# Attention and two MoE layers on one core: queries and keys of a pair interleaved on even and odd partitions

## The chip, the cores and the metric

One core of a Trainium2 chip runs the whole program. The metric is the device time of one execution in microseconds; 1132.95 us is the median of three runs before the change (1131.27, 1132.95 and 1136.18).

The engines are named as in the profile: PE multiplies matrices, DVE, ACT and POOL work on tiles, and SP issues most of the DMAs. [...]

## The reference

```python
def _attn_ref(q, k, v):                      # (4, 8, 576, 64) each, float32
    ...
    q_rot, k_rot = (rotate(q), rotate(k))    # x1*cos - x2*sin, x1*sin + x2*cos
    scores = scale * np.matmul(q_rot, k_rot.transpose(0, 1, 3, 2))
    scores = scores - np.max(scores, axis=-1, keepdims=True)
    attn = np.exp(scores)
    attn = attn / (np.sum(attn, axis=-1, keepdims=True) + 1e-09)
    return np.matmul(attn, v)

def _moe_ref(x, w_in, w_out, s, b):          # 2304 tokens, 512 -> 2048 -> 512
    r = np.maximum(x @ w_in, 0.0)
    return (s * (r * r) + b) @ w_out

def _moe2_ref(x, w_gate, w_val, w_out):      # 512 -> 1536 -> 512
    g = x @ w_gate
    return (g / (1.0 + np.exp(-g)) * (x @ w_val)) @ w_out
```

Attention's output, with the heads side by side, goes through the first layer and then through the second. The weights come as 64-bit floats and are decoded on the chip.

## The kernel before

**Precision.** Every 32-bit operand of a product is split into a high part (rounded to the PE's fast 32-bit format) and a low part (what is left). A product is then two or three matmuls: high by high, high by low, low by high.

**Attention** runs over 16 pairs of heads. For a pair p there are two jobs.

*Preparation* (`prep`, L425). SP loads the queries and keys of the two heads into a tile `x` (L392) and the values into `vr`. POOL applies the rotation in four instructions per pair: two products into a second tile `ry` (L486, L488), one product in place on `x` (L491), and the sum back into `x` (L494). (For pair 0 DVE does it, in three groups.) PE transposes the rotated `x` in three groups of three blocks (L514), so that queries lie on partitions 0 to 63 and keys on 64 to 127 of the PSUM tile `pst`. ACT writes the high part of each group into `qkhi` (L523), and DVE the low part into `qklo` (L525). Then SP copies the parts from SBUF to SBUF to where the score matmuls want them, ten "spreads" a pair (L547): into `a` (query high on the upper half of the partitions, query low on the lower half), `t` (key low above, key high below) and `kz` (key high above, zeros below). One matmul over 128 partitions of `a` and `t` then gives two of the three terms at once, and one of `a` and `kz` the third. Pairs 0 and 1 go without spreads: ACT and DVE write `a`, `t` and `kz` directly (L533, L536).

*The pair itself* (`pair`, L584). For each of nine blocks of 128 queries: four or eight score matmuls (L619), the row maximum on DVE (L622), the exponential on ACT (L626). Then, in three thirds, transposes of the exponentials (L680, L683), their high part on ACT (L688) and low part on DVE (L695), and the products with the values (L710, L712), whose result is stored to `x_d` (L731): high and low sums as two DMAs.

**The buffers that matter here.** `a`, `t`, `kz` exist twice, by the pair's parity, so the spreads of pair p can go only when the scores of pair p-2 are done. `qkhi` and `qklo` exist once: `qkhi` of pair p+1 can be written only when all ten spreads of pair p have landed. `ry` exists once, `x` twice, and `x` is free for a load when the transposes have read it.

**What sets the order.** The kernel records all operations with a duration, a priority and the buffers they take, and a list scheduler (`Schedule.run`, L70) emits them engine by engine in the order of its own clock. A pair's preparation has a priority of 2.4 pairs ahead, so the buffers decide when it comes. Once emitted, the order on an engine is fixed, and what the chip does later than the scheduler's clock said shows as a wait of the whole engine.

**The MoE layers** follow: first layer in five blocks of 512 or 384 tokens, second layer in three blocks, both with weights in a pool of slots: ten slots (`wa`) filled during attention and 22 (`WB`) that take the place of attention's tiles when these are given up.

## Time and profile before

| | us |
|---|---|
| median of three runs | 1132.95 |
| span of the profiled execution (first to last instruction) | 1130.5 |
| PE busy | 1103.6 |
| DVE busy | 801.2 |
| ACT busy | 591.0 |
| POOL busy | 193.0 |

The profile gives the profiled execution's span alone; the median of the runs is 2.45 us above it. The first matmuls of the MoE layers start at 305.0 us of the span, while attention's last pair runs out; the second layer's first activation is at 708.1 us. Matmuls overlap in the records, so a busy PE is not a PE at its peak, but an idle PE is idle.

How to read rows of waits: "PE ps_t L680 <- DVE qklo L525: 4.0, 2, 2.6" says that PE instructions of line 680 (they write tile `ps_t`) stood still for 4.0 us in total, twice, 2.6 us at the longest, until a DVE instruction of line 525 had ended. In a timeline the wait stands in brackets behind the instruction. Where one instruction waits for several events, the profile names the last one it knows of; a DMA named there can be another on the same queue.

### The profile page before, as it was taken

The page shows a single profiled execution, that of the slowest core. Times are in us where ns is not written, and L with a number is a line of the kernel's source. Part 1 is how long each engine was busy: PE and PEld are TensorE (multiplying, and loading weights), DVE is VectorE, ACT ScalarE, POOL GpSimd, SP SyncE. Part 2 cuts the span into 40 slices and gives each one's busy share as a digit, 9 for nine tenths or more (in the row PEclk, how much of TensorE's full clock was granted, in tenths as well). Part 3 has the DMA queues.
Part 4 walks back from the last instruction along what each step waited for, and adds up shares of the span by engine and source line. Part 5 has one row for each costly group of instructions (what it writes and reads, how often), then busy time and mean ns, then how long its engine had stood idle before and what let it go on. Part 6 is the DMA issues. An engine that isn't in the chain of part 4 may idle for free. (4 is left out here: it accounts for less than half of the span.)

```text
span 1130.5 us, 17993 instructions
## 1 busy us (share of the span) xinstructions
PE 1103.6 (98%) x6314; PEld 1006.8 (89%) x6314; DVE 801.2 (71%) x1391; ACT 591.0 (52%) x1199; POOL 193.0 (17%) x156
## 2 busy tenths in 40 slices
PE   8989989999999999999999999999999999999998
PEld 7889888989988788888899999999979999899986
DVE  5879788999979867868768764555565555655560
ACT  5979888889978845544554543322242222422230
POOL 6876775752210000000000000000000000000000
PEclk9899999999999999999999999999999999999999
DMA  5587978777375477576576766766646652666501
GB/s 117 128 208 175 240 184 213 175 184 185 89 235 185 128 227 235 177 238 225 198 241 212 254 224 207 245 204 204 210 160 220 196 195 97 196 229 197 181 10 46
DMA packets 185721, 211.16 MB, mean 187 GB/s; under 512 B 71824, under 2 KB 121120, under 8 KB 185632
## 3 DMA queue, kind: packets, MB, share of 16 engines
q1 hardware_dynamic: 183792, 209.23, 61.8%
q8 instruction: 50, 0.82, 0.3%
q10 hardware_dynamic: 1840, 0.79, 0.2%
q14 instruction: 39, 0.32, 0.1%
HBM read 142.07 MB, written 47.26 MB: 167 GB/s over the span
## 5 line engine op out<-in xcount | busy, mean ns | idle before, releaser
L1241 DVE TENSOR_TENSOR tmp<-hb,tmp 128x384 f32<-128x384 f32 x252 | 140.0, 557 | 113.3 <-PE hb L811 112.4
L811 PE MATMUL hb<-xh,w 128*128 128x384 f32 (+1 forms) x560 | 199.2, 356 | 1.0 <-DVE w L349 1.0
L809 PE MATMUL hb<-xh,w 128*128 128x384 f32 (+1 forms) x560 | 199.0, 355 | 0.3 <-DVE pl L695 0.3
L810 PE MATMUL hb<-xl,w 128*128 128x384 f32 (+1 forms) x560 | 198.8, 355 | 0.0
L809 PE MATMUL acc<-gh,w 128*128 128x512 f32 (+1 forms) x320 | 117.8, 368 | 0.0
L810 PE MATMUL acc<-gl,w 128*128 128x512 f32 (+1 forms) x320 | 117.6, 368 | 0.0
L811 PE MATMUL acc<-gh,w 128*128 128x512 f32 (+1 forms) x320 | 117.6, 367 | 0.0
L622 DVE TENSOR_REDUCE nm<-ps_s 128x1 f32<-128x576 f32 x144 | 108.0, 751 | 9.8 <-PE ps_s L619 8.6
L809 PEld LDWEIGHTS hb<-xh,w 128*128 128x128 f32 x560 | 105.1, 188 | 10.9 <-PE ps_t L683 0.5
L810 PEld LDWEIGHTS hb<-xl,w 128*128 128x128 f32 x560 | 105.1, 188 | 10.3
L811 PEld LDWEIGHTS hb<-xh,w 128*128 128x128 f32 x560 | 105.1, 188 | 9.8 <-DVE w L349 1.8
L626 ACT ACTIVATE e<-ps_s,nm 128x576 f32<-128x576 f32 x144 | 107.3, 746 | 8.4 <-DVE nm L622 7.8
L688 ACT ACTIVATE ph<-ps_t 128x512 fp32r<-128x512 f32 x192 | 106.2, 574 | 10.1 <-PE ps_t L680 7.8
L619 PE MATMUL ps_s<-t,a 128*128 128x288 f32 x320 | 101.2, 332 | 7.2 <-ACT e L626 7.0
L710 PE MATMUL ps_av<-ph,vh 128*128 128x384 f32 (+1 forms) x320 | 97.9, 327 | 0.7 <-ACT xr L723 0.6
L695 DVE TENSOR_TENSOR pl<-ps_t,ph 128x512 fp32r<-128x512 f32 x144 | 95.9, 683 | 2.5 <-ACT ph L688 1.4
L1256 ACT ACTIVATE tmp<-tmp 128x384 f32<-128x384 f32 x72 | 37.8, 525 | 111.1 <-DVE tmp L1241 108.9
L680 PE MATMUL ps_t<-ident,e 128*128 128x128 f32 x576 | 87.7, 279 | 5.6 <-DVE qklo L525 4.0
L619 PE MATMUL ps_s<-kz,a 128*128 128x288 f32 x320 | 90.8, 299 | 0.0
L810 PE MATMUL hb<-w 128*128 128x384 f32 x264 | 88.9, 337 | 0.0
L811 PE MATMUL hb<-w 128*128 128x384 f32 x264 | 88.8, 337 | 0.0
L809 PE MATMUL hb<-w 128*128 128x384 f32 x264 | 88.5, 335 | 0.0
(117 smaller groups left out, 2304.2 us busy)
## 6 DMA issues: line engine op xcount, KB each, us to landing
w<-wd SPq DMA_DIRECT2D x120, 512.0 KB, 4.3
wd<-w SPq DMA_DIRECT2D x48, 512.0 KB, 3.6
raw<-in_moe_w_out_dram SPq DMA_DIRECT2D x28, 512.0 KB, 4.1
x_d<-xr SPq DMA_DIRECT2D x64, 144.0 KB, 2.7
w<-wd SPq DMA_DIRECT2D x36, 256.0 KB, 3.6
raw<-in_moe_w_in_dram SPq DMA_DIRECT2D x16, 512.0 KB, 4.4
raw<-in_moe_w_gate_dram SPq DMA_DIRECT2D x12, 512.0 KB, 5.5
raw<-in_moe_w_val_dram SPq DMA_DIRECT2D x12, 512.0 KB, 6.6
```

What stands on the lines that cost most here:

```text
L619: nc.tensor.matmul(ps[:, hf * 512:hf * 512 + HS], a[:, q0:q0 + 128], m[:, k0:k0 + HS], start=y == 0, stop=y == len(todo) - 1)
L622: nc.vector.tensor_reduce(out=st["nm"][:, u:u + 1], in_=st["s", u], axis=AX.XY, op=ALU.max, negate=True)
L626: nc.scalar.activation(out=st["e", u].rearrange("p (f n) -> p f n", f=2), in_=st["s", u], func=AF.Exp, bias=st["nm"][:, u:u + 1], accum_ou ...
L680: nc.tensor.transpose(ps[:, z * 128:z * 128 + 128], st["e", u][:, kc * 128:kc * 128 + 128], ident)
L688: nc.scalar.activation(out=st["ph", y][0:rows, 512 * i:512 * i + n], in_=st["pt", y, i][0:rows, 0:n], func=AF.Copy)
L695: nc.vector.tensor_tensor(out=dst, in0=st["pt", y, i][0:rows, 0:n], in1=st["ph", y][0:rows, c].bitcast(F32), op=ALU.subtract)
L710: nc.tensor.matmul(ps, vv, st["ph", y][:, c], start=kc == 0, stop=kc == 4)
L809: nc.tensor.matmul(o, lh, rh, start=first, stop=False)
L810: nc.tensor.matmul(o, lh, rl, start=False, stop=False)
L811: nc.tensor.matmul(o, ll, rh, start=False, stop=last)
L1241: nc.vector.tensor_tensor(out=st[dst, f], in0=ps[z], in1=st[a, f], op=ALU.add)
L1256: nc.scalar.activation(out=st[key, f], in_=st[key, f], func=AF.Silu)
```

## The change

1. **Layout.** The sum of the rotation goes to `ry` instead of back to `x`, and for pairs 2 to 15 with the query and the key of a dimension next to each other (`"p c (a d j)"`). After the transpose queries lie on even partitions and keys on odd ones. `qkhi`, `qklo`, `a`, `t` and `kz` all get one width, 1216 columns, with a gap of 64 zero columns in the middle, and a spread copies every second partition whole: five DMAs of 64 x 1216 in place of ten of 64 x 576.
2. **Buffers.** `qkhi` and `qklo` exist twice, by parity (`hi0`, `hi1`); `ry` exists twice; `x` is free after the sum instead of after the transposes. `x` is laid out query first, key second, so a load writes 2304 contiguous bytes a partition instead of nine pieces of 256.
3. **Tables.** Only cosine and sine are loaded; ACT makes the negated sine and a second cosine (six instructions). The scale column is loaded with the identity matrix, and two POOL memsets go.
4. **Clearing.** Before the first spread into each `kz` (pairs 2 and 3) POOL clears the whole tile; four small memsets clear the gaps.
5. **Values and store.** High and low parts of the values are interleaved (POOL writes every second element), so high and low sums of a head come out on neighbouring partitions and are stored with one DMA of 128 partitions in place of two of 64.
6. **Start.** For pairs 1 and up POOL's rotation waits until DVE has done pair 0's.
7. **Slots.** 24 instead of 22 weight slots, from the space that was saved.

```diff
-    WB = 22
+    WB = 24
...
-        "raw": 3, "dec": 2, "wa": WA, "x": 2, "vr": 2, "ry": 1, "hi": 1, "vh": 3, ...
+        "raw": 3, "dec": 2, "wa": WA, "x": 2, "vr": 2, "ry": 2, "hi0": 1, "hi1": 1, "vh": 3, ...
...
+    SP = 2 * S + 64
+    a_t = [at_c.tile([128, SP], F32R, name=f"a{z}") for z in range(2)]
+    t_t = [at_c.tile([128, SP], F32R, name=f"t{z}") for z in range(2)]
+    kz_t = [at_c.tile([128, SP], F32R, name=f"kz{z}") for z in range(2)]
+    hi_t = [at_c.tile([128, SP], F32R, name=f"qkhi{z}") for z in range(2)]
+    lo_t = [at_c.tile([128, SP], F32R, name=f"qklo{z}") for z in range(2)]
...
-                    st["x"] = ld_p.tile([128, PC, 2, D], F32, tag="x", name="x")
+                    st["x"] = ld_p.tile([128, 2, PC, D], F32, tag="x", name="x")
...
+        rt_op.append(op("act", ..., lambda cs=cs: nc.scalar.activation(out=rt[:, cs, 3], in_=rt[:, cs, 2], func=AF.Copy, scale=-1.0), ...))
+        rt_op.append(op("act", ..., lambda cs=cs: nc.scalar.activation(out=rt[:, cs, 0], in_=rt[:, cs, 1], func=AF.Copy), ...))
...
+        def take_ry():
+            st["ryt"] = rp_p.tile([128, PC, 2 * D], F32, tag="ry", name="ry")
+            st["ry"] = st["ryt"].rearrange("p c (a d j) -> p j c a d" if p > 1 else "p c (j a d) -> p j c a d", j=2, a=2)
...
                 def y3():
-                    xv = st["x"].rearrange("p c j d -> p (c j d)")
-                    nc.gpsimd.tensor_tensor(out=xv, in0=xv, in1=st["ry"].rearrange("p c j a d -> p (c j a d)"), op=ALU.add)
+                    rv = st["ry"].rearrange("p j c a d -> p j c (a d)")
+                    nc.gpsimd.tensor_tensor(out=rv, in0=st["x"], in1=rv, op=ALU.add)
...
-                    o = op("pool", ..., fn, pr, (o, *lds[0], *rt_op), (ry_tok,) if y == 0 else (), (ry_tok,) if y == 3 else ())
+                    o = op("pool", ..., fn, pr, (o, *lds[0], *rt_op, *first_rope), (ry_tok,) if y == 0 else (), (x_tok,) if y == 3 else ())
...
-                    if g == 0:
-                        st["hi"] = rp_p.tile([128, 2 * S], F32R, tag="hi", name="qkhi")
-                        st["lo"] = rp_p.tile([128, 2 * S], F32R, tag="lo", name="qklo")
-                    nc.scalar.activation(out=place(st["hi"], g), in_=taken(st["ps", g]), func=AF.Copy, scale=qs_t)
+                    nc.scalar.activation(out=place(hi_x, g), in_=taken(st["ps", g]), func=AF.Copy, scale=qs_t)
...
+            cleared = ()
+            if p < 4:
+                cleared = (op("pool", t_pool1(SP), lambda: nc.gpsimd.memset(kz.bitcast(F32), 0.0), pr + 6, trs[:1], (tok,)),)
...
+            ev, od = slice(0, 128, 2), slice(1, 128, 2)
+            ops = [
+                sp(a[ev], hi_x[ev], p > 3),
+                sp(a[od], lo_x[ev]),
+                sp(t[ev], lo_x[od]),
+                sp(t[od], hi_x[od]),
+                sp(kz[ev], hi_x[od]),
+            ]
...
+            def part(j, h):
+                return st["vh"][j].rearrange("p c (d h) -> p c h d", h=2)[:, :, h]
...
-            for half in range(2):
-                def put(half=half):
-                    nc.sync.dma_start(out=x_d[half][b][128 * pp + 64 * j:128 * pp + 64 * j + 64], in_=st["xr"][64 * half:64 * half + 64, S * j:S * j + S])
+            def put():
+                nc.sync.dma_start(out=x_d[b][256 * pp + 128 * j:256 * pp + 128 * j + 128], in_=st["xr"][:, S * j:S * j + S])
```

The lines behind the change move by 4 to 14 (the spread is L561 after, the high part on ACT L534, the rotation on POOL L498, L500, L503 and L506, its values L583 and L585).

**Order on ACT around the high parts of pair 8** (three `qkhi` rows; `e` is an exponential, `ph` a high part of transposed exponentials, `xr` a sum taken from PSUM). Before:

```order
L688 ACTIVATE ph_1960<-ps_t_1978 128x512
L626 ACTIVATE e_1998,l_1371<-ps_s_1955,nm_1908 128x576
L626 ACTIVATE e_2015,l_1371<-ps_s_1989,nm_1908 128x576
L723 ACTIVATE xr_1928<-ps_av_1941 128x384
L688 ACTIVATE ph_1960<-ps_t_2017 64x384
L523 ACTIVATE qkhi_2047<-pst_2037,qs_203 128x2x192
L523 ACTIVATE qkhi_2047<-pst_2043,qs_203 128x2x192
L626 ACTIVATE e_2066,l_1371<-ps_s_2021,nm_1908 128x576
L523 ACTIVATE qkhi_2047<-pst_2050,qs_203 128x2x192
```

And after:

```order
L702 ACTIVATE ph_1775<-ps_t_1783 128x512
L640 ACTIVATE e_1800,l_1368<-ps_s_1768,nm_1615 128x576
L534 ACTIVATE qkhi0_205<-pst_1802,ident_197 128x2x192
L534 ACTIVATE qkhi0_205<-pst_1808,ident_197 128x2x192
L640 ACTIVATE e_1833,l_1368<-ps_s_1794,nm_1615 128x576
L534 ACTIVATE qkhi0_205<-pst_1817,ident_197 128x2x192
L737 ACTIVATE xr_1672<-ps_av_1757 128x384
```

Counted from the program's start, 58 exponentials stand ahead of the first `qkhi` row before and 51 after, 0.8 of a pair earlier, and the tile written is that of pair 6 instead of that of pair 7.

**Order on SP around the spreads of pair 7** (`qkhi`, `qklo` to `a1`, `t1`, `kz1`; `x_d` are stores of sums, `rbx` loads for the first layer). Before:

```order
L731 DMA x_d01_127<-xr_1658 64x576
L547 DMA a1_205<-qkhi_1774 64x576
L547 DMA a1_205<-qklo_1775 64x576
L547 DMA a1_205<-qkhi_1774 64x576
L547 DMA a1_205<-qklo_1775 64x576
L547 DMA t1_207<-qkhi_1774 64x576
L547 DMA t1_207<-qklo_1775 64x576
L547 DMA kz1_209<-qkhi_1774 64x576
L547 DMA t1_207<-qkhi_1774 64x576
L547 DMA t1_207<-qklo_1775 64x576
L547 DMA kz1_209<-qkhi_1774 64x576
L731 DMA x_d11_131<-xr_1658 64x576
```

And after:

```order
L561 DMA a1_200<-qkhi1_206 64x1216
L561 DMA a1_200<-qklo1_208 64x1216
L561 DMA t1_202<-qklo1_208 64x1216
L561 DMA t1_202<-qkhi1_206 64x1216
L561 DMA kz1_204<-qkhi1_206 64x1216
```

Five issues go from SP's queue here, and one more wherever a sum is stored.

**Order on POOL while it rotates pairs 2 and 3** (`x`, `ry` and `vh`, the values' parts). Before:

```order
L491 TENSOR_TENSOR x_356<-x_356,rt_202 128x1152
L494 TENSOR_TENSOR x_356<-x_356,ry_467 128x1152
L486 TENSOR_TENSOR ry_594<-x_506,rt_202 128x18x32
L488 TENSOR_TENSOR ry_594<-x_506,rt_202 128x18x32
L569 TENSOR_SCALAR vh_648<-vr_302 128x5x64
L491 TENSOR_TENSOR x_506<-x_506,rt_202 128x1152
L571 TENSOR_TENSOR vh_648<-vr_302,vh_648 128x5x64
L494 TENSOR_TENSOR x_506<-x_506,ry_594 128x1152
```

And after:

```order
L506 TENSOR_TENSOR ry_411<-x_347,ry_411 128x2x576
L498 TENSOR_TENSOR ry_575<-x_466,rt_198 128x2x9x32
L583 TENSOR_SCALAR vh_600<-vr_312 128x320
L500 TENSOR_TENSOR ry_575<-x_466,rt_198 128x2x9x32
L558 MEMSET kz0_203 128x1216
L503 TENSOR_TENSOR x_466<-x_466,rt_198 128x1152
L585 TENSOR_TENSOR vh_600<-vr_312,vh_600 128x320
L506 TENSOR_TENSOR ry_575<-x_466,ry_575 128x2x576
L583 TENSOR_SCALAR vh_749<-vr_312 128x320
```

The memset of `kz0`, which waits for pair 0's scores, stands inside pair 3's rotation, and the values' split that waited for a free `vh` tile stands behind that rotation instead of within it.

## Rows read from the trace of the kernel before

**Rows 1.** The page: busy time, share of the span, instructions; granted clock in tenths.
```profile
PE 1103.6 (98%) x6314; PEld 1006.8 (89%) x6314; DVE 801.2 (71%) x1391; ACT 591.0 (52%) x1199; POOL 193.0 (17%) x156
...
PEclk9899999999999999999999999999999999999999
```

**Rows 2.** Busy time by stretch: stretch, its length, then each engine (instructions); clock, DMA.
```profile
25.00:50.00 25.00, 22.53 (x156) 21.15 (x155) 21.18 (x35) 22.30 (x51) 19.60 (x13) 0.86 0.46 102
...
250.00:275.00 25.00, 24.98 (x188) 22.96 (x187) 24.59 (x41) 23.58 (x57) 7.01 (x8) 1.00 0.70 175
600.00:700.00 100.00, 100.00 (x579) 100.00 (x578) 70.30 (x126) 47.57 (x86) 0.00 (x0) 1.00 0.68 226
...
106.00:123.00 17.00, 16.97 (x133) 16.07 (x132) 15.51 (x26) 15.24 (x39) 10.14 (x8) 1.00 0.96 274
124.00:163.00 39.00, 33.31 (x251) 30.49 (x250) 30.76 (x49) 29.87 (x73) 30.16 (x27) 1.00 0.81 192
```

**Rows 3.** What PE waited for, 40 to 300 us: us in total, times, longest.
```profile
PE ps_s L619 <- ACT e L626: 4.1, 7, 2.0
PE ps_t L680 <- DVE qklo L525: 4.0, 2, 2.6
PE pst L514 <- DVE qklo L525: 2.2, 2, 1.9
PE psr L646 <- DVE qklo L525: 0.9, 1, 0.9
```

**Rows 4.** Timeline, two of the stalls: start, duration, engine, instruction, idle before it.
```profile
78.75 0.59 SPq L547 DMA_DIRECT2D kz<-qkhi  x1
...
82.00 1.05 ACT L523 ACTIVATE qkhi<-pst,qs 128x384 fp32r<-128x384 f32 x2 [2.56 <-DMA x_d<-xr]
...
132.37 0.60 SPq L547 DMA_DIRECT2D kz<-qkhi  x1
...
135.20 1.05 ACT L523 ACTIVATE qkhi<-pst,qs 128x384 fp32r<-128x384 f32 x2 [4.01 <-DMA kz<-qkhi]
135.82 1.15 DVE L525 SCALAR_TENSOR_TENSOR qklo<-pst,qs,qkhi 128x384 fp32r<-128x384 f32 x2 [3.25 <-ACT qkhi L523]
...
136.49 0.96 PE L680 MATMUL ps_t<-ident,e 128*128 128x128 f32 x6 [2.63 <-DVE qklo L525]
```

**Rows 5.** The spreads' line: issue time in ns (min/median/max), and time to landing.
```profile
L547 SPq DMA_DIRECT2D kz<-qkhi x28: 462/596/1337, 46.0 to 277.1; - x28
...
DMA to landing us min/median/max: 2.4/3.2/7.6
```

**Rows 6.** POOL, 55 to 300 us: its busy time, and groups (busy, mean ns, idle before).
```profile
55.00:300.00 245.00, 147.33 (x117) 1.00 0.78 188
...
L494 POOL TENSOR_TENSOR x<-x,ry 128x1152 f32<-128x1152 f32 x12 | 31.9, 2659 | 0.8
...
L571 POOL TENSOR_TENSOR vh<-vr,vh 128x320 fp32r<-128x320 f32 x27 | 24.7, 914 | 1.5
...
L486 POOL TENSOR_TENSOR ry<-x,rt 128x576 f32<-128x576 f32 x11 | 15.6, 1421 | 20.4 <-DMA x<-in_k_dram 19.1 <-issue 1.3
L569 POOL TENSOR_SCALAR vh<-vr 128x320 fp32r<-128x320 f32 x27 | 14.2, 525 | 46.1 <-PE ps_av L710 46.1
```

**Rows 7.** ACT by line, 512 elements: every second word read (L304), and contiguous (L342).
```profile
L304 ACT ACTIVATE dec<-raw x68: 649/668/744, 157.6 to 651.9; 128x512 f32<-128x512 f32 x68
...
L342 ACT ACTIVATE w<-dec x44: 612/626/676, 226.8 to 655.8; 128x512 fp32r<-128x512 f32 x44
```

**Rows 8.** What PE waited for behind attention, 300 us to the end.
```profile
PE acc L1173 <- ACT o L1190: 2.0, 2, 1.3
PE hb L811 <- DVE w L349: 1.0, 2, 0.5
```

**Rows 9.** POOL memsets at the start, and POOL's idle time near 40 us.
```profile
L381 POOL MEMSET kz<- x2: 1054/1054/1054, 1.0 to 2.3; 64x1152 f32 x2
...
39.92 0.46 POOL L569 TENSOR_SCALAR vh<-vr 128x320 fp32r<-128x320 f32 x1 [4.57 <-PE ps_av L710]
```

More of the change, by code (lines that the diff above doesn't have):

```diff
@@ L249, in tile_attention_moe_moe @@
     vr_p = att.enter_context(tc.tile_pool(name="vr", bufs=2))
-    rp_p = att.enter_context(tc.tile_pool(name="rp", bufs=1))
+    rp_p = att.enter_context(tc.tile_pool(name="rp", bufs=2))
     v_p = att.enter_context(tc.tile_pool(name="v", bufs=3))
@@ L254, in tile_attention_moe_moe @@
     e_p = att.enter_context(tc.tile_pool(name="e", bufs=NE))
-    x_d = [[dram.tile([DM, S], F32, name=f"x_d{half}{b}") for b in range(B)] for half in range(2)]
+    x_d = [dram.tile([2 * DM, S], F32, name=f"x_d{b}") for b in range(B)]
     r_d = [dram.tile([H // 2, 2 * S], F32, name=f"r_d{b}") for b in range(B)]
@@ L262, in tile_attention_moe_moe, with table @@
     bv = const.tile([128, 1], F32, name="bv")
-    ident = at_c.tile([128, 128], F32, name="ident")
-    rt = at_c.tile([128, PC, 3, D // 2], F32, name="rt")
-    qs_t = at_c.tile([128, 1], F32, name="qs")
-    a_t = [at_c.tile([128, 2 * S + 128], F32R, name=f"a{z}") for z in range(2)]
-    t_t = [at_c.tile([128, 2 * S], F32R, name=f"t{z}") for z in range(2)]
-    kz_t = [at_c.tile([128, 2 * S], F32R, name=f"kz{z}") for z in range(2)]
+    ident_qs = at_c.tile([128, 129], F32, name="ident")
+    ident, qs_t = ident_qs[:, 0:128], ident_qs[:, 128:129]
+    rt = at_c.tile([128, PC, 4, D // 2], F32, name="rt")
+    def table(a, n, c0, c1):
+        x = rt[:, c0:c1, a:a + n].rearrange("p c a d -> p c (a d)")
+        return bass.AP(x.tensor, x.offset, [list(x.ap[0]), [0, 2], *(list(y) for y in x.ap[1:])])
+    SP = 2 * S + 64
[4 more added lines that the diff above has]
+    lo_t = [at_c.tile([128, SP], F32R, name=f"qklo{z}") for z in range(2)]
     def dma(o, i, size, prio, after=()):
@@ L365, in tile_attention_moe_moe, with place @@
     spread_op = {}
-    def a_pieces(c0, c1):
-        if c0 < S:
-            yield c0, min(c1, S), c0
-        if c1 > S:
-            yield max(c0, S), c1, max(c0, S) + 64
-    def place(x, g, gap=0):
+    def place(x, g):
         c = S // G
-        return x.rearrange("p (h s) -> p h s", h=2)[:, :, g * c:(g + 1) * c]
+        s = g * c
+        w = S + 64
+        return bass.AP(x.tensor, x.offset + s, [list(x.ap[0]), [w, 2], [1, c]])
+    gaps = []
     def zero(z, prio):
         o0 = op("pool", 0.2, lambda: nc.gpsimd.memset(a_t[z][:, S:S + 64].bitcast(F32), 0.0), prio)
+        for x in (hi_t[z], lo_t[z]):
+            gaps.append(op("pool", 0.2, lambda x=x: nc.gpsimd.memset(x[:, S:S + 64].bitcast(F32), 0.0), -250))
         o1 = op("pool", 1.0, lambda: nc.gpsimd.memset(kz_t[z][64:128].bitcast(F32), 0.0), prio)
@@ L389, in ld @@
                 if "x" not in st:
[L390 removed]
+                    st["x"] = ld_p.tile([128, 2, PC, D], F32, tag="x", name="x")
                 c = slice(g0 * PC // G, g1 * PC // G)
                 (nc.scalar if p == 0 and (j or g0 == 0) else nc.sync).dma_start(
[L393 removed]
+                    out=st["x"][:, j, c, :],
                     in_=src[b, h0:h0 + 2].rearrange("h s d -> (h s) d").rearrange("(p c) d -> p c d", p=128)[:, c],
@@ L500, in prep @@
               o = None
-              for y, fn in enumerate((r0, r1, r2, r3)):
-                deps = [o, *lds[g], rt_op[g]]
+              for y, fn in enumerate((r1, r0, r2, r3)):
+                deps = [o, *lds[g], (rt_ld[g], rt_op[2 * g], rt_op[2 * g + 1], None)[y]]
                 if y == 0 and g > 0:
@@ L616, in s_mm @@
                 for hf in range(2):
-                    todo = [(q0, k0 + hf * HS, m) for q0, k0 in terms for m in (t, kz)]
+                    todo = [(q0, (S + 64 if k0 else 0) + hf * HS, m) for q0, k0 in terms for m in (t, kz)]
                     for y, (q0, k0, m) in enumerate(todo):
@@ L933, in block_b @@
         for o, m, b, s in x_pieces(sum(UBS[:j]), UB, S):
-            pieces.append((o, m, (x_d[0][b][:, s:s + m], x_d[1][b][:, s:s + m])))
+            pieces.append((o, m, tuple(x_d[b].rearrange("(f h) t -> h f t", h=2)[h, :, s:s + m] for h in range(2))))
             batches.append((b, s, m, o))
@@ L1340, in _tables @@
     cos, sin = np.cos(freqs), np.sin(freqs)
-    one = np.stack([cos, sin, -sin], axis=1).astype(np.float32)
+    one = np.stack([cos, sin], axis=1).astype(np.float32)
     rows = np.concatenate([one, one], axis=0)
-    rows = rows.reshape(128, rows.shape[0] // 128, 3, half)
-    return np.ascontiguousarray(rows), np.eye(128, dtype=np.float32)
+    rows = rows.reshape(128, rows.shape[0] // 128, 2, half)
+    scale = np.where(np.arange(128) % 2, 1.0, D ** -0.5).astype(np.float32)
+    return np.ascontiguousarray(rows), np.concatenate([np.eye(128, dtype=np.float32), scale[:, None]], axis=1)
 def kernel(**inputs):
```

91 lines of the change are left out of this document (41 added, 50 removed).

## The prediction

> **What bounds the kernel now.** I read the page first. PE is busy for 98% of the span [rows 1], so nothing in this change can pay unless it fills a hole on PE; DVE, ACT and POOL are far lower on average. The change touches attention and, by the two extra slots, the MoE layers, so the second view is busy time by stretch. In the MoE stretch 600 to 700 us PE is busy 100.00 of 100.00 us [rows 2], and behind 300 us its waits come to a few us in all [rows 8]: there is nothing to gain there. In attention two stretches differ. From 106 to 123 us PE is busy 16.97 of 17.00 us; from 124 to 163 us it is busy 33.31 of 39.00 us, and in the same stretch DVE and ACT also stand idle for over 8 us each [rows 2]. All three idle together means a chain, not a full engine. Third view, who PE waited for between 40 and 300 us: most of it is "DVE qklo" (4.0 + 2.2 + 0.9 us), and one wait of 2.0 us for an exponential [rows 3]. Fourth, the timeline there. At 132.37 us SP issues the last spread of one pair; at 135.20 us, 2.83 us later, ACT writes the next pair's `qkhi` after standing 4.01 us; DVE's `qklo` follows at 135.82 (3.25 us idle), PE's transposes at 136.49 (2.63 us idle) [rows 4]. At 78.75 and 82.00 us it is the same picture, 3.25 us apart [rows 4]. The spreads' median time to landing is 3.2 us [rows 5]. So the releaser is the landing of the previous pair's last spread, also where the row names a store on the same queue: `qkhi` is a single tile, ACT stands in order behind it, the exponentials and DVE stand behind ACT, and PE behind both.
>
> **The change part by part.**
>
> *Two `qkhi` and `qklo` tiles.* This takes the cause away. Pair p's high part now waits for the spreads of pair p-2. Before pair 8's first high part the program has 51 exponentials where it had 58, so pair 8 is handled when about 5.7 pairs are through; pair 6's spreads, which wait for pair 4's scores, are free to go at 5.0. A pair takes about 17 us (the undisturbed stretch of rows 2 is one), so there are some 12 us between the two. The spreads need five issues of 0.6 us and 3.2 us to land [rows 5], 6.2 us, so some 5 us are left. The price: the DVE waits, 4.0 + 2.2 + 0.9 = 7.1 us, less 0.3 us for the one short wait among them (2.2 in two, the longest 1.9), plus the 2.0 us wait for an exponential, which I put down to the same cause: 8.8 us [rows 3]. Of the other exponential waits, 4.1 - 2.0 = 2.1 us in six [rows 3], I take half as the tail of the same stalls: 1.0 us. Bounds: 7 us (the exponential waits stay) to 11 us. Does it come through? In the bad stretch ACT idles 9.1 and DVE 8.2 us of 39, PE 5.7 [rows 2], so neither of the others was full while PE waited, and the time is PE's. What is late next is DVE: in a stall-free stretch at 250 to 275 us it is busy 24.59 of 25.00 us, and PE 24.98 [rows 2]. Both are then full, so I count nothing beyond the waits.
>
> *Five spreads for ten, one store for two.* Bytes go from 10 x 144 KB to 5 x 304 KB, 5% more; issues fall by five and two a pair. At 0.6 us [rows 5] SP saves about 4 us a pair. No engine waits for SP as such; it lets loads go earlier. Cover: PE's waits for a spread do not show among the larger rows [rows 3]. I count 0, bounds 0 to 2 us of gain.
>
> [...]
>
> *Loads of `x` in long pieces, `x` free sooner, two `ry`.* POOL idles 19.1 us before rotations that wait for such a load [rows 6]. PE never waits for POOL in attention [rows 3], so this is 0 on the path; it makes the earlier preparation possible.
>
> *POOL's work.* The same number of elements, but each `ry` and `vh` write now steps by two words. From 55 to 300 us POOL is busy 147.33 of 245.00 us [rows 6], 60%. Touched are the two products into `ry` (1.42 us each), the sum (2.66), and per head the values' two halves (0.53 + 0.91): 2.84 + 2.66 + 2.88 = 8.4 us a pair. No row shows POOL stepping. The nearest is ACT reading every second word, 0.668 against 0.626 us, 7% [rows 7]; that would be 0.6 us a pair beside some 40% of POOL's time idle (98 of 245 us), so 0. The other end is under the rivals.
>
> *Two clears of `kz` and four small memsets.* 1.05 us for 64 x 1152 [rows 9], so about 1.1 us each. `kz0`'s stands on POOL in pair 3's rotation and waits for pair 0's scores; behind it wait that rotation and pair 2's spreads. POOL had 4.57 us idle just behind that place [rows 9], for a value split that now stands further back. I count 0; if that cover were gone, 1.1 us each, 2 us.
>
> *Start.* Six small ACT copies come before the first high parts, and pair 1's rotation on POOL waits for pair 0's on DVE. Shorter loads speak for a gain, the copies against; both are below 1 us by the size of the work, and I count 0, bounds -1 to +1. [...]
>
> *24 slots.* They can only fetch weights earlier. PE waited 1.0 us for a weight [rows 8]: 0, bounds 0 to 1 us of gain. The reordering in these layers could cost about as much as those waits, 1 to 2 us.
>
> **The sum.** 8.8 + 1.0 = 9.8 us off. The profiled execution's span of 1130.5 us becomes 1120.7. The median of the runs stands 2.45 us above that span, and I carry that over: 1123 us.
>
> **The rivals.**
>
> *A. The stalls move instead of going.* For pairs 11 and 12 the distance between the spreads of two pairs before and the high parts is smaller (the order has their first `qkhi` at 8.4 and 9.4 pairs, and the spreads are free at 8.0 and 9.0). 0.4 pair is 7 us, of which 6.2 us are needed, and SP may have other issues queued in front. With one such stall of 2.6 us in each of these pairs and the half-saturated DVE eating another microsecond or two, half the gain is left: 1128 us. For it: the scheduler's clock was too early about the landings before too. Against: the five fewer issues.
>
> *B. POOL becomes the bound (slower side).* If a stepped write costs POOL much more, the rotation comes late and PE waits for transposes. POOL has 147.33 us of work in 245.00 us [rows 6], with about 14 pairs in them, 10.5 us a pair of 17.5. It decides from the point where 8.4 us of touched work have grown by 7, by 83%. If they take 2.5 times as long, POOL needs 10.5 + 12.6 = 23.1 us a pair; over 14 pairs that is 5.6 x 14 = 78 us, less a lead of about a pair: some 60 us on top, 1183 us. At twice as long it is 18.9 us a pair, 1.4 x 14 = 20 us, nearly eaten by the lead: 1130 to 1143. For it: no row shows such a write on POOL. Against: the 7% on ACT, far from 83%, for which I give B no more than 0.10. [...]
>
> *C. More than the waits comes back.* If the shorter queue, the earlier loads and the clock in 25 to 50 us (0.86, so 3.5 us of 25 lost at most [rows 2]) all improve, another 4 to 8 us go: 1117 us.
>
> **How the numbers follow.** Forecast, 1119 to 1127 us: 0.48. A, 1127 to 1133: 0.22. C, 1110 to 1119: 0.20. B, above 1139: 0.10. Half a per cent, about what can be told from no change, is 5.7 us, so the limits are 1127.3 and 1138.6. Faster is the forecast and C: 0.68. Same is A: 0.22. Slower is B: 0.10. The range from 1113 to 1132 leaves out B, the tail of A and the far half of C.
>
> **What would show it.** In the changed profile ACT's `qkhi` rows should have no idle time of more than about 0.5 us ahead of them, "DVE qklo" should be gone from PE's waits, and the stretch 124 to 163 us should have PE busy above 38 of 39 us. POOL's `ry` and `vh` rows should keep their durations within 10%. I am wrong if `qkhi` still waits for a DMA, if the PE idle time comes back under another name (exponentials, `x` loads, `a` of pair 1), or if POOL's rows have grown by more than half.

## The result, and the profile after

The changed kernel takes 1121.03 us (median; 1120.08 to 1122.55, 4 runs), the kernel before beside it 1132.36 us (1131.27 to 1136.18, 4 runs). The ratio is 0.9897 with a 95% interval of 0.9874 to 0.992: faster by 1.0%, 11.3 us. The forecast was 1123 us. The time came out within 2 us of it, but the experiments below show that the gain does not hang on the part of the change to which the prediction gave it.

The profiled execution has a span of 1118.3 us, 12.2 us less than before. Its time by stretch, with the columns of [rows 2]:

```profile
25.00:50.00 25.00, 21.98 (x159) 20.73 (x158) 22.00 (x36) 22.98 (x54) 20.20 (x15) 0.93 0.45 150
124.00:163.00 39.00, 36.62 (x287) 34.81 (x286) 37.01 (x57) 34.28 (x83) 31.09 (x27) 1.00 0.65 215
250.00:275.00 25.00, 24.09 (x181) 22.47 (x180) 23.87 (x40) 23.79 (x56) 9.40 (x10) 1.00 0.58 202
600.00:700.00 100.00, 100.00 (x578) 100.00 (x578) 64.17 (x114) 47.24 (x86) 0.00 (x0) 1.00 0.70 234
```

The MoE stretch is full as it was. In 124 to 163 us PE is busy 36.62 of 39.00 us where it had 33.31 [rows 2]. The last two columns of such a row are the mean busy share of the DMA engines and the GB/s that they moved, and they are the ones that I had passed over; the column ahead of them is PE's granted clock, which in the trace of either kernel stands at one of two levels, 1.00 and 0.50 (a figure between them is an average over both). Over nearly all of attention they read in the kernel before:

```profile
50.00:290.00 240.00, 227.14 (x1722) 211.93 (x1721) 216.53 (x345) 208.05 (x495) 149.65 (x117) 1.00 0.80 192
```

and in the changed kernel:

```profile
50.00:290.00 240.00, 233.73 (x1803) 221.18 (x1801) 229.02 (x367) 221.01 (x523) 155.93 (x124) 1.00 0.58 196
```

The DMA engines move as much (192 and 196 GB/s) and are busy 0.58 of the time instead of 0.80.

What PE waits for in the changed kernel, 40 to 290 us (us in total, times, longest), against [rows 3]:

```profile
PE ps_av L724 <- DVE ph L709: 2.2, 1, 2.2
PE ps_s L633 <- ACT e L640: 1.9, 4, 0.7
PE ps_av L724 <- ACT xr L737: 1.0, 2, 0.7
PE ps_t L694 <- DVE qklo L536: 0.3, 1, 0.3
```

The waits that ended in `qklo` are down from 7.1 to 0.3 us, those for an exponential from 4.1 to 1.9. The line of `qkhi` itself, L534 now, shows why (instruction, duration min/median/max in ns, and what ended its engine's idle time):

```profile
L534 ACT ACTIVATE qkhi<-pst,ident x42: 570/582/608, 36.3 to 237.5; 128x384 fp32r<-128x384 f32 x42
L534 ACTq EVENT_SEMAPHORE  x25: 17/17/38, 35.6 to 235.0; - x25
...
  PE pst L527: 0.2, 1
```

No semaphore takes longer than 38 ns and no transfer is among the releasers; in [rows 4] there stood 4.01 us of ACT's idle time behind the landing of `kz`. One new stall has come. On the timeline (start, duration; both engines):

```profile
154.63 3.26 DVE L318 SCALAR_TENSOR_TENSOR dec<-raw,dec 128x512 uint32<-128x512 uint32 x1
...
154.64 2.71 POOL L506 TENSOR_TENSOR ry<-x,ry 128x1152 f32<-128x1152 f32 x1
```

A weight's decoding on DVE takes 3.26 us where its median is 0.692 us, beside a rotation's sum on POOL that began 0.01 us after it. `ph` is late by that, and it is the 2.2 us in PE's first row above.

A finer account than the waits, read from the timelines: the first score matmul starts at 14.64 us (13.98 before), from there to the end of the last `ps_av` matmul it takes 285.6 us (301.0), and the rest 818.0 us (815.6). So 15.4 us went in attention, and some 3 came back at its two ends. The last border is soft, since MoE matmuls run before it too.

A second account splits the 12.2 us of the span by PE's idle and busy time. PE's busy time on the page was 1103.6 us [rows 1] and is now 1096.1:

```profile
PE 1096.1 (98%) x6314; PEld 1002.8 (90%) x6314; DVE 799.2 (71%) x1391; ACT 592.8 (53%) x1205; POOL 193.9 (17%) x160
```

So PE is idle for 22.2 us where it was idle for 26.9, 4.7 us less, and busy for 7.5 us less with the same 6314 matmuls. From 50 to 290 us, where the waits lie, its idle time fell by 6.6 us (12.86 to 6.27). Of the busy time, the clock explains a part: between 15 and 40 us the granted clock was at its lower level, 0.50, for 10.2 us before and for 3.4 us after, and 6.8 us at half the clock are worth some 3.4 us (an estimate from these numbers). The other 4 us or so are not accounted for. Nor is the clock's part peculiar to this execution: the granted clock, averaged over the span, was 0.996 to 0.998 in the four executions of the changed kernel, and 0.995 (median) in the 39 of the kernel before that were run beside the experiments.

### The profile page after: what moved, and what is told of

Read it like the earlier page. It is cut to its first block, busy times and chain, and to the rows that moved or that the text cites. A ratio compares the mean times of both kernels' runs of the same rounds, so it can differ in the third digit from the quotient of the medians.

```text
span 1118.3 us, 17806 instructions
## 1 busy us (share of the span) xinstructions
PE 1096.1 (98%) x6314; PEld 1002.8 (90%) x6314; DVE 799.2 (71%) x1391; ACT 592.8 (53%) x1205; POOL 193.9 (17%) x160
## 2 busy tenths in 40 slices
DMA packets 148119, 212.14 MB, mean 190 GB/s; under 512 B 34480, under 2 KB 84160, under 8 KB 148032
## 5 line engine op out<-in xcount | busy, mean ns | idle before, releaser
L823 PEld LDWEIGHTS hb<-xl,w 128*128 128x128 f32 x560 | 105.1, 188 | 10.4
## 6 DMA issues: line engine op xcount, KB each, us to landing
x_d<-xr SPq DMA_DIRECT2D x32, 288.0 KB, 2.5
```

The source lines that it names most:

```text
L823: nc.tensor.matmul(o, lh, rl, start=False, stop=False)
```

## The experiments

The table has every run: the median of the runs, the ratio to the kernel before with its interval, then, from the profiled execution, the time from the first score matmul to the end of the last `ps_av` matmul ("attention") and the DMA share from 50 to 290 us.

| run | us | ratio (95%) | attention, us | DMA share |
|---|---|---|---|---|
| before | 1132.4 | 1 | 301.0 | 0.80 |
| after | 1121.0 | 0.9897 (0.9874 to 0.992) | 285.6 | 0.58 |
| one_hi | 1120.0 | 0.9883 (0.9864 to 0.9903) | 288.0 | 0.58 |
| one_ry | 1118.3 | 0.9873 (0.9855 to 0.9892) | 286.1 | 0.58 |
| one_both | 1118.2 | 0.9873 (0.986 to 0.9886) | 286.9 | 0.58 |
| two_hi | 1136.4 | 1.0027 (1.0016 to 1.0038) | 303.3 | 0.78 |
| half_spreads | 1128.6 | 0.9957 (0.9941 to 0.9974) | 291.4 | 0.76 |
| ten_spreads | 1122.3 | 0.989 (0.9874 to 0.9906) | 286.6 | 0.61 |
| tiny_issues | 1129.8 | 0.9961 (0.9947 to 0.9975) | 296.6 | 0.61 |
| halves_kept | 1125.6 | 0.9939 (0.992 to 0.9957) | 294.1 | 0.72 |
| five_before | 1135.6 | 1.0027 (1.0015 to 1.0039) | 306.0 | 0.81 |
| few_before | 1143.7 | 1.0074 (1.0052 to 1.0097) | 300.5 | 0.80 |
| five_store_before | 1142.1 | 1.0077 (1.0065 to 1.0089) | 303.3 | 0.78 |
| wb22 | 1121.8 | 0.9887 (0.9873 to 0.9902) | 289.3 | 0.59 |

The attention column is one execution each and is no firmer than that: wb22 runs the changed kernel's program unchanged throughout attention, and its execution is 3.7 us longer there.

### Is it the second tiles?

**One pair of `qkhi`/`qklo` tiles in the changed kernel.**

```diff
-"hi0": 1, "hi1": 1
+"hi0": 1
-Token(f"hi{z}")
+Token("hi0")
-hi_x, lo_x = hi_t[z], lo_t[z]
+hi_x, lo_x = hi_t[0], lo_t[0]
```

> The changed kernel with one qkhi/qklo pair of tiles in place of two; all else of the change stays (five spreads over all partitions, one store a head, x freed after the sum, two ry, 24 slots). Theory T (the gain is the second pair of tiles): ACT's qkhi again waits for the landing of the pair before's last spread, the row with the longest wait rises from 0.04 us to 2 us or more, PE's waits that end in qklo come back with 4 to 8 us in 40 to 290 us, and the time is 1127 to 1131 us. Rival S (five short spreads carry the gain; with them one tile would land in time): qkhi's longest wait stays below 1 us and the time is 1121 to 1124 us. Rival L (the earlier freeing of x and the second ry carry it): the same, 1121 to 1124 us.

1120.0 us, not slower than the changed kernel, and no PE wait between 32 and 300 us ends in `qklo`. `qkhi`'s longest semaphore is 38 ns, as with two tiles. My theory T has fallen: the changed kernel does not need the second pair. This is not because the second pair stands unused there. In the changed kernel 10 of the 13 high parts that follow another pair's are begun before that pair's first spread is even issued, which one tile would forbid. For pair 8's, between the last spread of pair 6 and the first of pair 7:

```profile
101.86 0.60 SPq L561 DMA_DIRECT2D kz<-qkhi  x1
...
113.24 1.05 ACT L534 ACTIVATE qkhi<-pst,ident 128x384 fp32r<-128x384 f32 x2
...
117.62 0.54 SPq L561 DMA_DIRECT2D a<-qkhi  x1
```

With one tile the program puts the high part behind the spreads again; in one_hi pair 8's, behind the last spread of pair 7:

```profile
122.38 0.60 SPq L561 DMA_DIRECT2D kz<-qkhi  x1
...
127.28 0.58 ACT L534 ACTIVATE qkhi<-pst,ident 128x384 fp32r<-128x384 f32 x1
```

That costs nothing because the spreads are through sooner. From a pair's first spread to the next pair's first high part it is 9.2 us (median) in one_hi and 9.3 in the kernel before; but from the first issue to the last landing it is 5.9 us in one_hi and 9.5 in the kernel before (medians of the pairs whose last landing the trace has, 11 and 5 of 14).

**The second pair alone, in the kernel before.**

```diff
-"hi": 1,
+"hi0": 1, "hi1": 1,
-Token("hi")
+Token(f"hi{z}")
-tag="hi", name="qkhi"
+tag=f"hi{z}", name="qkhi"
-tag="lo", name="qklo"
+tag=f"lo{z}", name="qklo"
-num_devices=1)
+num_devices=1, dynamic_dma_scratch_size=1024)
```

> The kernel before with two qkhi/qklo pairs of tiles and nothing else of the change (ten spreads over halves of the partitions, two stores a head, one ry, x held until the transposes; the space comes from a smaller scratch area for DMA descriptors, which this kernel does not use). Theory T: PE's waits that end in qklo (7.1 us in 40 to 300 us before) fall below 2 us and the time is 1122 to 1126 us. Rivals S and L: the high part is earlier free but ten spreads or the single ry keep the preparation where it was, PE's waits that end in qklo stay at 4 us or more or turn up at the transposes, and the time is 1129 to 1133 us.

1136.4 us: 0.3% slower than before. The stall has moved, not gone. On its timeline, the last spread of pair 7 and the first high part of pair 9, which now waits for that one:

```profile
135.52 0.59 SPq L547 DMA_DIRECT2D kz<-qkhi  x1
...
139.26 1.05 ACT L523 ACTIVATE qkhi<-pst,qs 128x384 fp32r<-128x384 f32 x2 [7.86 <-DMA x_d<-xr]
...
140.55 1.12 PE L680 MATMUL ps_t<-ident,e 128*128 128x128 f32 x4 [7.50 <-DVE qklo L525]
```

The row names a store on the same queue; the spread landed at 139.03 us, 0.23 us before. With the second tile the program puts the high parts earlier, the spreads of two pairs before land no sooner (3.4 to 4.0 us, medians; 2.9 to 3.3 in the kernel before), and one wait of 7.50 us on PE is what comes of it. This is the prediction's rival A, in the kernel where the spreads are still slow.

**One `ry`, and one of both.**

```diff
-"ry": 2,
+"ry": 1,
-tc.tile_pool(name="rp", bufs=2)
+tc.tile_pool(name="rp", bufs=1)
```

> The changed kernel with one ry tile in place of two. The rotation of a pair must then wait on POOL until the transposes of the pair before have read ry. Theory T: POOL has some 40 per cent of idle time, so it waits longer and PE notices at most 1 to 2 us: 1120 to 1123 us. Rival L (the lead that the second ry gives is what fills PE): waits on PE at the transposes or behind qklo of 5 us or more, 1126 to 1131 us.

> The changed kernel with one ry and one qkhi/qklo pair of tiles at once. Theory Q: with five issues a pair neither second buffer is needed, 1117 to 1121 us. Rival E (either of the two gives the lead that the other would, so that taking one away showed nothing): qkhi waits for a spread again or PE for the transposes, 1126 us or more.

1118.3 and 1118.2 us (one_both is this diff with that of one_hi). Neither second buffer is needed, nor one in place of the other; rivals L and E have fallen. Both medians lie some 3 us below the changed kernel's, with intervals that overlap its interval, so I call them not slower. Of those 3 us a part can be seen at the start. With two `ry`, POOL takes up pair 1's rotation while DVE still rotates pair 0; the changed kernel:

```profile
11.06 1.16 DVE L493 TENSOR_TENSOR ry<-x,ry 128x384 f32<-128x384 f32 x1
...
10.40 1.40 POOL L498 TENSOR_TENSOR ry<-x,rt 128x576 f32<-128x576 f32 x1 [6.52 <-DMA x<-in_k_dram]
```

and one_ry:

```profile
11.01 0.56 DVE L493 TENSOR_TENSOR ry<-x,ry 128x384 f32<-128x384 f32 x1
...
13.10 1.40 POOL L498 TENSOR_TENSOR ry<-x,rt 128x576 f32<-128x576 f32 x1
```

The one DVE sum that overlaps POOL's product takes 1.16 us instead of 0.56, and the first score matmul starts at 14.64 us instead of 13.99. Part 6 of the change was to keep the two apart. It orders them in the scheduler's clock alone: in the changed kernel POOL's product starts at 10.40 us, before DVE's last sum has begun, and what it waited for was its load.

### Layout or number of the spreads?

The next three kernels give PE, ACT, DVE and POOL the same instructions in the same order as one another; they differ only in what SP issues for a pair's spreads. In half_spreads and ten_spreads there are ten issues of 152 KB each, cut by partitions or by columns.

```diff
-            ev, od = slice(0, 128, 2), slice(1, 128, 2)
+            for r0 in (0, 64):
+                ev, od = slice(r0, r0 + 64, 2), slice(r0 + 1, r0 + 64, 2)
```
```diff
-                sp(a[ev], hi_x[ev], p > 3),
+            for c in (slice(0, SP // 2), slice(SP // 2, SP)):
+                    sp(a[ev, c], hi_x[ev, c], p > 3 and c.start == 0),
...
```

> The changed kernel with each of the five spreads cut into two over partitions 0 to 63 and 64 to 127, so ten issues of 152 KB over halves, as before in number and halves; the interleaved layout stays. Theory T: nobody on the path waits for a spread, five more issues of 0.6 us a pair cost SP 3 us a pair, PE notices nothing: 1120 to 1123 us. Rival S: the spreads' length and number count; the last one lands 3 us or more later, the waits for t or kz come up in PE's waits and the time is 1125 us or more.

> The changed kernel with each of the five spreads cut into two by columns: ten issues, but each over all partitions. Theory Q: as half_spreads, 1126 to 1130 us, since SP issues as many. Rival P: it was the halves of the partitions that cost half_spreads its 7 us; by columns the time is 1120 to 1123 us.

1128.6 and 1122.3 us, with intervals far apart (0.9941 to 0.9974 and 0.9874 to 0.9906). Same number, same bytes, same order: the halves of the partitions alone cost 6.3 us by the medians and 7.6 us by the ratios. The transfers (KB each, median us from issue to landing), half_spreads:

```profile
a<-qkhi SPq DMA_DIRECT2D x26, 152.0 KB, 3.4
...
kz<-qkhi SPq DMA_DIRECT2D x26, 152.0 KB, 3.8
```

and ten_spreads:

```profile
a<-qkhi SPq DMA_DIRECT2D x26, 152.0 KB, 2.1
...
kz<-qkhi SPq DMA_DIRECT2D x26, 152.0 KB, 2.2
```

The trace lists every packet: one of 4864 bytes takes 379 ns (median) in half_spreads and 191 ns in the changed kernel, twice as long for the same row. Over the whole stretch the DMA share is 0.76 and 0.61. PE's longest wait is at the same place in both traces, near 183 us. It is not the wait that the prediction had priced. That one comes up once in half_spreads, in front of pair 9's high part, with 1.47 us of ACT's idle time behind a semaphore that ends when a spread of pair 7 lands (ten_spreads has none):

```profile
L534 ACTq EVENT_SEMAPHORE  x36: 17/38/2594, 35.2 to 239.8; - x36
```

PE's waits that end in `qklo` are 1.5 us there and 0.4 us in ten_spreads. At the longest wait POOL's `xs` waits for the load of the sums (`rbx`), which stands on the queue behind the spreads, ACT's `xh` waits for `xs`, and behind `xh` on ACT stand the exponentials. half_spreads:

```profile
184.57 0.72 POOL L807 TENSOR_TENSOR xs<-xs,rbx 128x256 f32<-128x256 f32 x1 [2.50 <-DMA rbx<-r_d]
...
185.33 0.63 ACT L811 ACTIVATE xh<-xs 128x512 fp32r<-128x512 f32 x1 [5.29 <-POOL xs L807]
```

ten_spreads:

```profile
183.31 0.63 ACT L811 ACTIVATE xh<-xs 128x512 fp32r<-128x512 f32 x1 [3.06 <-POOL xs L807]
```

PE's wait behind it is 4.8 us in the one and 2.5 us in the other. In half_spreads the granted clock fell during that wait, and PE's first 5.1 us of work behind it ran at the lower level, 0.50; in ten_spreads it stayed at 1.00. The 5.1 us behind the wait, with the columns of [rows 2], half_spreads:

```profile
187.20:192.30 5.10, 5.08 (x21) 4.97 (x22) 3.93 (x6) 3.25 (x8) 0.15 (x1) 0.50 0.28 64
```

and ten_spreads:

```profile
185.20:190.30 5.10, 5.10 (x40) 4.99 (x40) 4.91 (x9) 5.09 (x13) 2.35 (x3) 1.00 0.37 97
```

PE runs 21 matmuls in the one and 40 in the other, so the late load costs 2.3 us of waiting and some 2.5 us of clock (an estimate, half of 5.1). The two profiled executions, 1124.75 and 1120.64 us, are 4.1 us apart, less than the medians are.

Why a packet of a transfer over half of the partitions takes twice as long (379 against 191 ns), no run shows.

**Five tiny transfers more, in the same order.**

```diff
+            for y in range(5):
+                ops.append(sch.dma(
+                    8192, lambda y=y: nc.sync.dma_start(out=a[0:8, S + 8 * y:S + 8 * y + 8].bitcast(F32), in_=hi_x[0:8, S + 8 * y:S + 8 * y + 8].bitcast(F32)),
...
```

> The changed kernel with five more transfers a pair behind the five spreads, each of 8 partitions by 32 bytes of zeros: as many issues on SP's queue as in the run half_spreads (some 160 us of issue in 50 to 290 us, where the changed kernel has 116.8 and the kernel before 190.7), but no more bytes and no other layout. Theory Q (SP's queue works in order and its issues were what the kernel before ran short of; fewer issues are the gain): it costs like half_spreads, 1126 to 1130 us. Rival P (the spreads over all partitions are faster in the DMA engines, the number of issues does not count): 1120 to 1122 us. Rival T, the second pair of tiles, has fallen with the runs one_hi and two_hi and expects 1120 to 1122 us here.

1129.8 us, the value of theory Q, but not for its reason. The five write into columns of `a` that the spreads also write, so SP stands until those have landed (SP's waits, 50 to 290 us: us in total, times, longest):

```profile
SPq L574 <- DMA a<-qklo: 9.8, 10, 1.5
```

This run therefore held the queue still, which ten_spreads with as many issues does not. It shows only that holding up what stands behind the spreads on SP's queue cost as much here (1129.8 us) as slow spreads did in half_spreads (1128.6 us). On the number of issues it says nothing.

**Halves, in the changed kernel's own order.**

```diff
-                return sch.dma(
-                    256 * SP, lambda: nc.sync.dma_start(out=o.bitcast(F32), in_=i.bitcast(F32)), pr + 6,
+                def fn():
+                    for r in (slice(0, 32), slice(32, 64)):
+                        nc.sync.dma_start(out=o[r].bitcast(F32), in_=i[r].bitcast(F32))
+                return sch.dma(
+                    256 * SP, fn, pr + 6,
```

> The changed kernel with every spread issued as two, over partitions 0 to 63 and 64 to 127, in the place of the one: ten issues a pair, and the order of every instruction on PE, ACT, DVE and POOL kept. With two qkhi tiles no high part waits for them; what stands behind them on SP (x, v, the loads of sums and weights) comes 3 us later in each pair. Theory Q: ACT or DVE wait in order for one of those, PE loses 3 to 8 us, 1124 to 1129 us. Rival N (half_spreads and tiny_issues lost their 7 us by the new order that came with them, not by the issues): 1120 to 1122.5 us.

1125.6 us; by the ratios (0.9939 and 0.9897) 4.8 us above the changed kernel. The four engines' order is that of the changed kernel, so it is not a new order that costs (rival N). In the profiled execution (1128.1 us, among the longer of six that run from 1122.3 to 1129.0) nearly all of it is one wait. A weight's load was issued at 136.38 us in the changed kernel; here, on the timeline of SP and ACT:

```profile
144.71 0.45 SPq L299 DMA_DIRECT2D raw<-in_moe_w_in_dram  x1
...
149.95 0.66 ACT L312 ACTIVATE dec<-raw 128x512 f32<-128x512 f32 x1 [4.91 <-DMA raw<-in_moe_w_in_dram]
```

It left 8.3 us later, ACT stood for 4.91 us in front of its decoding with the exponentials behind it, and PE waited 4.2 us in one piece; the 5.0 us behind that ran at the lower level of the clock, 0.50. `qkhi` waits for no transfer here either. Here both ten issues and halves were at work; which of them cost how much this run can't tell.

### Fewer issues in the kernel before

**Ten spreads issued as five, still over halves, order kept.**

```diff
-            for s0, s1, d0 in a_pieces(0, 2 * S):
...
+            for y in range(2):
+                ops.append(sp(two(a[0:64]), lambda: h2(st["hi"][0:64]), True if y == 0 else None, S))
+                ops.append(sp(two(a[64:128]), lambda: h2(st["lo"][0:64]), False if y == 0 else None, S))
...
+                if first is not None:
+                    nc.sync.dma_start(out=o.bitcast(F32), in_=i().bitcast(F32))
```

(The second call of each pair issues nothing; the first takes the whole width.)

> The kernel before with its ten spreads a pair issued as five, still over halves of the partitions and with the same bytes: a's two pieces in one issue, t's and kz's whole width in one. The order of every instruction on PE, ACT, DVE and POOL is kept as it was, so nothing is planned anew; only SP has five issues less a pair (some 70 of 300 in 50 to 290 us, about 42 of 190.7 us). Theory Q (the last of ten issues leaves 3 us later than the last of five, and qkhi, in order on ACT, waits for it): PE's waits that end in qklo fall from 7.1 us to below 3, and the time is 1124 to 1128 us. Rival P (it takes spreads over all partitions, halves land too late however few): the waits stay above 5 us, 1130 to 1134 us. Rival T (only a second tile helps): the same, 1130 to 1134 us.

1135.6 us, 0.3% slower than before. The five transfers of 288 KB take longer to land than the ten of 144 KB did (2.9 to 3.3 us), those into `a` 3.5 and 4.5 us and the others about twice as long:

```profile
t<-qkhi SPq DMA_DIRECT2D x13, 288.0 KB, 6.0
t<-qklo SPq DMA_DIRECT2D x13, 288.0 KB, 6.4
kz<-qkhi SPq DMA_DIRECT2D x13, 288.0 KB, 5.9
```

and `qkhi` waits for them more than before (what ended ACT's idle time ahead of L523, us and times):

```profile
  DMA kz<-qkhi: 14.1, 8
  PE pst L514: 5.2, 5
```

In the kernel before, 4.0 us ended at this transfer and 7.0 at others behind it on the queue (here 2.6). SP issues the last spread 2.4 us sooner, but the DMA engines are not done sooner; the DMA share is 0.81, where it was 0.80. Theory Q, that SP's issues were what ran short, has fallen. With half_spreads and ten_spreads this makes a square: ten issues over halves 1132.4 (before) or 1128.6 (half_spreads), five over halves 1135.6, ten over all partitions 1122.3, five over all 1121.0. Fewer issues bring nothing over halves and at most 1.3 us, inside the intervals, over all partitions; the layout does what is seen. The two times over all partitions are those of kernels with two tiles, though. With one tile the number may count: from a pair's first issue to its last landing it takes 9.5 us (before) or 10.1 (five_before) over halves, 8.2 over all partitions with ten issues (ten_spreads) and 5.9 with five (one_hi), and the high part comes 9.2 us behind the first issue. Ten spreads over all partitions with one tile were not run.

**Fewer issues with one store a head.**

```diff
-            for s0 in (0, S):
-                c = slice(s0, s0 + S)
+            for c in (slice(0, 2 * S),):
...
-            for half in range(2):
-                def put(half=half):
-                    nc.sync.dma_start(out=x_d[half][b][128 * pp + 64 * j:128 * pp + 64 * j + 64], in_=st["xr"][64 * half:64 * half + 64, S * j:S * j + S])
+            def put():
+                nc.sync.dma_start(out=x_d[b][256 * pp + 128 * j:256 * pp + 128 * j + 128], in_=st["xr"][:, S * j:S * j + S])
```

> The kernel before with fewer issues on SP and no other part of the change: t and kz by three spreads of the whole width in place of six, so seven spreads a pair over halves of the partitions, and one store a head in place of two. That takes some 66 of 300 issues away in 50 to 290 us, 190.7 us of issue become about 150. Theory Q: at about the issue time of half_spreads the time is 1124 to 1129 us, and PE's waits that end in qklo fall from 7.1 us to below 4. Rival P: the spreads still run over halves of the partitions, the time stays at 1130 to 1134 us.

> As five_before, and the raw sums of a head stored by one issue in place of two, order kept again. Theory Q: another 2 issues a pair, 1.2 us, of which the spreads that follow stores see a part: 0 to 2 us below five_before. Rivals P and T: 1130 to 1134 us, as five_before.

few_before: 1143.7 us, five_store_before (five_before with the store): 1142.1 us. Both totals carry a cost that I had put in myself: with the kernel before's layout a head's sums stored at once must be read back by twice as many loads over halves of the partitions, and from the last `ps_av` to the end these kernels need 829.1 and 822.7 us where the kernel before needs 815.6. Their attention, 300.5 and 303.3 us against 301.0, can be read: fewer issues and one store give nothing there that shows. The store's own price in the changed kernel, where no such loads are needed, stays open.

### The slots

```diff
-    WB = 24
+    WB = 22
```

> The changed kernel with 22 weight slots in place of 24. All theories of attention: no difference, 1120 to 1122 us, PE's losses behind 290 us within 1 us of those of the changed kernel. If the two slots do carry something, 1123 us or more with longer waits for w behind 600 us.

1121.8 us; the two slots carry nothing that can be measured.

## Why the prediction was right, and where it was not

**What was waited for** was right: the landing of the pair before's spreads, in front of `qkhi`, in front of everything on ACT. The waits priced at 8.8 us did go: `qklo` rows from 7.1 to 0.3 us, exponentials from 4.1 to 1.9.

**The time** was right, 1123 forecast and 1121.0 measured, and the range held it, but in part by luck. Other waits came in (3.2 us in front of `ps_av`), so that from 50 to 290 us PE's idle time fell by 6.6 us, not by the 9.8 of the sum. What brings the total back near the forecast is mostly the clock, some 3.4 us in the profiled executions (the estimate above), which the sum did not have.

**What removes it** was right for the wait and wrong for the gain. "This takes the cause away", said of the second pair of tiles: in the changed kernel the tiles do let the high parts run ahead, and even where the spreads are slow `qkhi` waits for one once (half_spreads, 1.5 us) or never (halves_kept). But quick spreads do away with the same wait without them (one_hi, one_both), so the gain does not hang on the tiles; and in the kernel before the tiles alone give nothing (two_hi). Whether they would be needed beside slow spreads was not run. The part of the change that cannot be taken back without loss is the one counted as "0, bounds 0 to 2 us of gain": spreads over all partitions. Without it 6.3 of the 11.3 us are gone (7.6 by the ratios) in the one comparison that changes nothing else, and 4.8 in halves_kept, which has more issues as well. They are lost mostly at waits that the sum did not have: a load of sums or of a weight that comes late behind slow spreads, and the clock behind that wait. The step failed at "No engine waits for SP as such": true of SP's issues (ten_spreads, five_before), but what stands behind the spreads on the queue waits for the DMA engines, and so did the `qkhi` of [rows 4], 4.01 us behind `kz`, a row that the prediction had in hand.

**"some 5 us are left"** between a pair's spreads and the high part two pairs on was more than enough in the changed kernel, from whose order it was worked out: pair 8's high part comes 11.4 us after the last spread of pair 6 was issued, and those of pairs 11 and 12, which rival A had named, 10.4 and 8.6 us after theirs. Rival A's mechanism came up where the spreads are slow: in two_hi, whose program also puts the high parts earlier, and once in half_spreads.

**POOL's stepped writes** at 0: right, and rival B is out. The sum into `ry`, the products, the values' two halves (busy, mean ns), against 2659, 1421, 914 and 525 ns in [rows 6]:

```profile
L506 POOL TENSOR_TENSOR ry<-x,ry 128x1152 f32<-128x1152 f32 x12 | 32.6, 2716 | 0.2
...
L585 POOL TENSOR_TENSOR vh<-vr,vh 128x320 fp32r<-128x320 f32 x28 | 25.5, 911 | 1.3
...
L498 POOL TENSOR_TENSOR ry<-x,rt 128x576 f32<-128x576 f32 x11 | 15.7, 1431 | 19.1 <-PE pst L527 14.3 <-DMA x<-in_q_dram 4.7
L583 POOL TENSOR_SCALAR vh<-vr 128x320 fp32r<-128x320 f32 x28 | 13.9, 495 | 38.8 <-PE ps_av L724 38.8
```

At most 2% more, far from the 83% from which rival B was to decide. (That sum divides POOL's work by 14 pairs, where the rows have 12 sums, so POOL had less room than 83%; at 2% it makes no difference. The bytes of the spreads rise by 5.6%, not by 5.)

**Of the signs that were named**, `qkhi` without idle time, `qklo` gone from PE's waits and POOL's rows within 10% came true. "PE busy above 38 of 39 us" in 124 to 163 us did not: 36.62, by the collision at 154.63 us that nobody forecast. **The start** was put at -1 to +1 us and cost 0.66 us, since POOL did not wait for DVE there. **The clock** between 25 and 50 us went from 0.86 to 0.93, a part of rival C that the sum had at nothing; what raised it is not shown. **The slots** at 0: right. **The reordering** behind attention was given 1 to 2 us; the rest behind the last `ps_av` is 2.4 us longer, which a soft border makes no firmer than that.

**What stays open.** half_spreads, with halves but all other parts of the change, still beats the kernel before by 0.4% (1128.6 us), 4 to 5 us. Which of the other parts does that isn't settled. `x` in long pieces is a candidate: packets under 512 bytes fall from 71,824 to 34,480, and `x` lands in 2.9 and 3.6 us instead of 3.8 and 4.5. So is the other order of the program. A kernel with `x` alone in short pieces was not run, nor halves with one tile, which would tell whether a second tile pays where the spreads are slow.

**A smaller version** came with the tests: one_both, with neither second buffer, at 1118.2 us (0.9873 of the kernel before), is not slower than the changed kernel and takes up less SBUF.

## What to carry to other kernels

A stall can be priced from its wait before one knows what will end it, so a forecast of the time can be near with the wrong reason. When a change has several parts, ask of each whether it shortens the wait or only lets something run ahead of it; two parts can each do away with the same wait, so undo them one at a time and look where the loss turns up, for it need not be the wait that was priced. Where the releaser in a wait is a transfer, read the DMA share and the GB/s of that stretch together: a high share at an ordinary rate (0.80 at 192 GB/s, 0.58 at 196) meant here that the shape of the transfers was at fault. And late transfers that nobody on the path needed yet became waits of the path here: a weight (4.91 us of ACT's time, 4.2 us of PE's, halves_kept) and a sum (5.29 and 4.8 us, half_spreads), since the exponentials stood behind them in ACT's order.

## What the runs showed of the hardware

- A transfer of 152 KB over 32 partitions of one half (every second one) landed in 3.4 to 3.8 us (half_spreads, medians), of the same bytes over every second partition of all 128 in 2.1 to 2.3 us (ten_spreads). Packets of 4864 bytes took 379 ns (half_spreads) and 191 ns (the changed kernel). Taking every second partition cost nothing that shows: at 191 ns for 4864 bytes these packets are as quick per byte as those of 2304 bytes (93 ns) of `x` and of the stores, over all 128 partitions without a step. Keeping to one half did cost, 379 against 191 ns.
- Five transfers of 288 KB over halves (five_before) landed no sooner than ten of 144 KB (the kernel before): the last was issued 2.4 us earlier and took 3 us longer (5.9 against 2.9 us for `kz`).
- PE's longer waits cost more than their length in these runs: the granted clock fell from 1.00 to 0.50 during those of 4.8 us (half_spreads), 4.2 us (halves_kept) and 7.5 us (two_hi), and the 5.1, 5.0 and 4.7 us of work behind them ran at 0.50. In ten_spreads, after 2.5 us, it stayed at 1.00. After 2.2 us it stayed there in the changed kernel and fell for 3.4 us in wb22.
- Two DVE instructions with two inputs in SBUF took longer beside one of POOL in the changed kernel: a decoding 3.26 us for a median of 0.69 beside a sum of 2.71 us, a rotation's sum 1.16 us beside a product of 1.40 us, where it takes 0.56 in one_ry without POOL beside it. What held them up, no run shows.
- POOL's writes of every second word took at most 2% longer than those of every word: 2716 against 2659 ns, 911 against 914, 495 against 525.
